# Attention and two mixing blocks on one core: transposes in half-row tiles, and jobs ordered by a table of ranks

## Chip, core and metric

The kernel runs on one NeuronCore of a Trainium2 chip. The metric is device time in microseconds (us), lower is better. The kernel before takes 760.67 us (median of 3 runs, 758.09 to 761.02).

## What is computed

The reference, cut to its three steps (4 batches, 12 heads, 448 positions, head size 64; all float32 but the weights, which come as float64):

```python
scores = scale * np.matmul(q, k.transpose(0, 1, 3, 2))
mask = np.triu(np.ones((seq, seq), dtype=bool), k=1)
...
attn = np.exp(scores)
attn = attn / (np.sum(attn, axis=-1, keepdims=True) + 1e-09)
...
h = np.maximum(xt @ w_tok1, 0.0) @ w_tok2
u = x + h.transpose(0, 2, 1)
h2 = np.maximum(u @ w_ch1, 0.0) @ w_ch2
...
h = np.maximum(x @ w_in, 0.0)
...
u, v = (h[..., :d_ff // 2], h[..., d_ff // 2:])
...
v_n = (v - mu) / np.sqrt(var + 1e-06)
v_s = np.einsum('ts,bsd->btd', w_spatial, v_n) + b_spatial[None, :, None]
gated = u * v_s
return (gated @ w_out).astype(np.float32)
```

## The kernel before, in words

**Jobs and the planner.** The kernel does not write out the order of its instructions. It makes a list of jobs, each with an engine, an estimated duration, the keys that it reads and writes, the buffers that it holds, and a priority (`Plan.job`, L110). `Plan.order` (L134) then simulates the engines (`run`, L197): whenever an engine is free, it takes of the ready jobs the one with the lowest priority value. It does so up to six times; after each pass `due` (L162) works out when each job has to be done at the latest, and these times are the priorities of the next pass. The best of the passes is emitted, and each engine and the one DMA queue (SyncE's, called SP) carries its jobs out in that order, so that a job that waits holds up those behind it on its engine. PSUM banks are given out in this simulation too.

**The stages.** The 48 heads are taken as 24 pairs, n = 0 to 23.
- *Attention.* `scores(n)` (L437) multiplies q and k of both heads of a pair (L497); one head's operands lie in partitions 0 to 63, the other's in 64 to 127, so that each matmul uses half of the array's rows. The queries go in four chunks of 64, 128, 128 and 128. VectorE adds the mask and takes the row maxima (L506), ScalarE takes the exponential and the row sums (L523), VectorE adds 1e-9 to the sums (L534) and inverts them (L535), GpSimd scales the rows (L544). The scores use banks 0 to 3.
- *Transposes.* For n < 17, `transposed(n)` (L553) turns the probabilities with TensorE (L581): 16 blocks of 128 x 128, four to a bank, and each bank is copied to SBUF by ScalarE (L585) or VectorE (L584). From n = 17 on `turned(n)` does it with VectorE and DMAs. The transposes, the weighted sum and the token mixing share banks 4 and 5 (for n < 6 also 6).
- *Weighted sum.* `weighted(n)` (L647) multiplies the turned probabilities with v (L683, L688), each matmul on half of the array's columns, two at once. The result goes to the tile U of the batch.
- *Token mixing* (`token_mix`, L718), after every third pair, and *channel mixing* (`channel`, L861, and for batches 2 and 3 `channel_pair`, L1040, which does seven products in place of eight). Every operand of these products is split in a high and a low float32r part, and a product takes three matmuls (`mm3`, L332: L336 to L338).
- *Gated part* (L1150 on): values, gate, spatial product, projection.

**Weights.** They are loaded as float64 (L381, L1105), turned to float32 by three integer operations on VectorE each (`narrow`, L340: L351, L353, L355), and stored to DRAM (L395, L1107), from where they are loaded again when they are used (L818, L984). The intermediate words lie in PSUM bank 7 for the first eight pieces of the channel weights, and then in bank 3.

## Time and profile before

| what | before |
|---|---|
| time, median of 3 runs | 760.67 us |
| span of the profiled execution | 760.7 us |
| TensorE (PE) busy | 747.2 us, 98% |
| VectorE (DVE) busy | 622.3 us, 82% |
| ScalarE (ACT) busy | 427.4 us, 56% |
| GpSimd (POOL) busy | 298.2 us, 39% |
| moved by DMA | 122.02 MB, mean 160 GB/s |

The profile is that of one execution; its times start at the span's beginning. PE stands for matmuls and PEld for weight loads, which overlap with them. A matmul's own duration is longer than its share of the engine, since matmuls are pipelined: what one costs is read from the start of one to the start of the next. In a timeline, equal instructions that follow each other stand in one line with their number.

### The profile page before, as it was taken

The numbers are of one execution on the slowest core, as the hardware profiler recorded it, in microseconds if no ns is written. First come the engines' busy times: TensorE is split into PE (matmuls) and PEld (weight loads), VectorE is DVE, ScalarE is ACT, GpSimd is POOL, SyncE is SP. The second block draws the span as 40 slices with busy tenths as digits, with TensorE's granted clock in tenths as the row PEclk, the third lists the DMA queues.
The fourth block names the chain that finished last, engine by engine and source line by source line (L and its number), as shares of the span: only waits on it lengthen the run. The fifth ranks groups of instructions, "written<-read, shape, count | busy, mean of one in ns | idle before, by whom it ended". The sixth has DMA issues, their size and how long they took to land. (4 is left out here: it accounts for less than half of the span.)

```text
span 760.7 us, 12440 instructions
## 1 busy us (share of the span) xinstructions
PE 747.2 (98%) x4216; PEld 640.3 (84%) x4216; DVE 622.3 (82%) x1512; ACT 427.4 (56%) x1040; POOL 298.2 (39%) x354
## 2 busy tenths in 40 slices
PE   8999999999989999999999999999999999999998
PEld 4577778888887888888889989998988888888997
DVE  6999599999867878876469978999999897599482
ACT  6998776445347765552336666654573665545241
POOL 4788764265494766563310000000420151542210
PEclk9999999999999999999999999999999999999999
DMA  6687158999976898898823122520301100400213
GB/s 228 207 285 238 55 163 316 335 318 333 339 225 190 298 307 250 234 304 220 241 84 117 39 84 84 187 84 1 118 22 42 43 0 1 132 1 28 83 49 133
DMA packets 48608, 122.02 MB, mean 160 GB/s; under 512 B 4896, under 2 KB 20256, under 8 KB 48032
## 3 DMA queue, kind: packets, MB, share of 16 engines
q1 hardware_dynamic: 48544, 121.23, 48.7%
q8 instruction: 33, 0.54, 0.3%
q14 instruction: 31, 0.25, 0.1%
HBM read 91.46 MB, written 29.75 MB: 159 GB/s over the span
## 5 line engine op out<-in xcount | busy, mean ns | idle before, releaser
L336 PE MATMUL psf<-fb,fa 128*128 128x448 f32 x420 | 154.0, 367 | 1.2 <-DVE hs L1001 0.6
L337 PE MATMUL psf<-fb,fa 128*128 128x448 f32 x420 | 153.7, 366 | 0.0
L338 PE MATMUL psf<-fb,fa 128*128 128x448 f32 x420 | 153.6, 366 | 0.0
L327 POOL TENSOR_TENSOR whl<-whl 128x768 fp32r<-128x768 f32 x45 | 83.2, 1851 | 89.5 <-ACT whl L819 89.4
L523 ACT ACTIVATE P<-P,stats 128x448 f32<-128x448 f32 (+3 forms) x192 | 96.1, 505 | 31.1 <-DVE stats L506 30.8
L544 POOL TENSOR_SCALAR P<-P,stats 128x448 f32<-128x448 f32 (+3 forms) x192 | 88.3, 483 | 38.1 <-DVE stats L535 30.8
L336 PEld LDWEIGHTS psf<-fb,fa 128*128 128x128 f32 x420 | 78.9, 188 | 9.2 <-DVE hs L1001 1.0
L337 PEld LDWEIGHTS psf<-fb,fa 128*128 128x128 f32 x420 | 78.9, 188 | 6.8
L338 PEld LDWEIGHTS psf<-fb,fa 128*128 128x128 f32 x420 | 78.9, 188 | 6.7
L506 DVE CUSTOM_DVE_ANT_0 P<-pss,mask 128x448 f32<-128x448 f32 (+3 forms) x192 | 70.9, 415 | 16.4 <-PE pss L497 16.0
L938 ACT CAST fa<-raw 128x384 fp32r<-128x384 f32 (+1 forms) x112 | 56.4, 531 | 42.7 <-DVE raw L951 21.6
L327 POOL TENSOR_TENSOR wv<-wf,wv 128x512 fp32r<-128x512 f32 x6 | 9.2, 1546 | 153.2 <-ACT wv L1156 153.2
L327 DVE TENSOR_TENSOR fa<-raw,fa 128x384 fp32r<-128x384 f32 (+1 forms) x109 | 61.0, 585 | 7.1 <-ACT fa L938 7.1
L336 PE MATMUL ps<-hid,whl 128*128 128x448 f32 x144 | 55.2, 383 | 3.1 <-DVE hid L330 1.9
L819 ACT CAST whl<-whl 128x768 fp32r<-128x768 f32 x45 | 37.4, 833 | 34.6 <-DMA whl<-plain 33.5
L336 PE MATMUL ps<-uhl,whl 128*128 128x448 f32 x144 | 55.6, 386 | 0.2 <-DVE U L859 0.2
L338 PE MATMUL ps<-hid,whl 128*128 128x448 f32 x144 | 53.3, 370 | 0.0
L337 PE MATMUL ps<-hid,whl 128*128 128x448 f32 x144 | 53.3, 370 | 0.0
L338 PE MATMUL ps<-uhl,whl 128*128 128x448 f32 x144 | 52.7, 366 | 0.0
L337 PE MATMUL ps<-uhl,whl 128*128 128x448 f32 x144 | 52.7, 366 | 0.0
L859 DVE TENSOR_TENSOR U<-ps,U 128x448 f32<-128x448 f32 x48 | 29.5, 619 | 20.9 <-PE ps L338 20.8
L327 POOL TENSOR_TENSOR ql<-stage,qh 128x896 fp32r<-128x896 f32 x18 | 38.1, 2116 | 14.9 <-issue 11.7
(174 smaller groups left out, 1793.2 us busy)
## 6 DMA issues: line engine op xcount, KB each, us to landing
way<-in_wch SPq DMA_DIRECT2D x24, 768.0 KB, 5.7
whl<-plain SPq DMA_DIRECT2D x45, 384.0 KB, 5.0
stage<-in_qkv SPq DMA_DIRECT2D x23, 448.0 KB, 4.7
plain<-way SPq DMA_DIRECT2D x24, 384.0 KB, 6.7
raw<-plain SPq DMA_DIRECT2D x24, 384.0 KB, 3.9
round<-PB SPq DMA_DIRECT2D x7, 1024.0 KB, 6.2
PT<-round SPq DMA_DIRECT2D x28, 256.0 KB, 6.2
v<-in_qkv SPq DMA_DIRECT2D x24, 256.0 KB, 4.1
```

Of the source, the lines that this page charges most:

```text
L327: e.tensor_tensor(lo, x, hi.bitcast(F32), op=ALU.subtract)
L336: nc.tensor.matmul(ps, ah, bh, start=(first and i == 0), stop=False, **kw)
L337: nc.tensor.matmul(ps, ah, bl, start=False, stop=False, **kw)
L338: nc.tensor.matmul(ps, al, bh, start=False, stop=(last and i == n - 1), **kw)
L506: nc.vector.tensor_tensor_reduce(out=P(i)[:M, j, :], in0=ps(i, j), in1=mask[:M, S - 128 : S - 128 + W] if j == 0 and n < BLOCKS or M == 64 ...
L523: nc.scalar.activation(P(i)[:M, j, :], P(i)[:M, j, :], AF.Exp, bias=s.t[:M, 0, c : c + 1], scale=-1.0, accum_out=s.t[:M, 1, c : c + 1])
L544: nc.gpsimd.tensor_scalar(P(i)[:M, j, :], P(i)[:M, j, :], s.t[:M, 2, c : c + 1], 1.0, op0=ALU.mult, op1=ALU.mult)
L819: job("ACT", act(DM, False), lambda: nc.scalar.copy(w.t[:, 0, :], w.t[:, 1, :].bitcast(F32)), r=ks, w=ks, prio=p)
L859: job("DVE", dve(S), lambda d=d, ps=ps: nc.vector.tensor_tensor(u.t[:, d, :], ps.t[:, :S], u.t[:, d, :], op=ALU.add), r=[(ps, 0), *u_keys( ...
L938: job("ACT", act(n, False), lambda: nc.scalar.copy(part(o, 0), at(d)), r=[key(d)], w=[wk], prio=p + 0.1 * o)
```

## The change

1. `transposed` makes two jobs per pair of heads in place of four. Each takes eight blocks, and turns each block in two halves: partitions 0 to 63 into one PSUM bank, partitions 64 to 127 into another, 64 columns each. In all 31 transposes of half a block replace 16 (the last block has one half). The four copies to SBUF have 512, 512, 512 and 448 columns, and write every second group of 64. `weighted` reads the new layout; its first product is cut in 384 and 64 columns.
2. `Plan.order` runs the simulation once, with priorities from a table of ranks that stands in the file, one for each job. The simulation has new durations and delays, counts a switch between full, half-row and half-column matmuls, and prefers to stay in one of these modes. `PASSES` and `due` are gone.
3. The float64 weights lie in DRAM so that each piece that a DMA loads is contiguous as a whole.
4. 1e-9 is put beside each row sum once, at the start, and a `tensor_reduce` adds the two, in place of `tensor_scalar_add`.
5. The conversion of the first eight pieces of channel weights can use bank 7 or 3.

The diff, cut to its core (new durations alone are left out):

```diff
+RANKS = (
...
     def order(self):
...
-        own = {j: (j.eng, j.us, j.emit, j.prio) for j in self.jobs}
-        best = None
-        for k in range(PASSES):
...
+        ranks = array("H", b85decode("".join(RANKS)))
+        assert len(ranks) == len(self.jobs)
+        for j, r in zip(self.jobs, ranks):
+            j.prio = r / 40
+        self.run()
         return sorted(self.jobs, key=lambda j: (j.start, j.index))
...
+            return min(((s, j) for s, j in starts if s <= first + NEAR), key=lambda x: (x[1].prio + (e == "PE" and x[1].mode != mode) * STAY, x[1].index))
...
+            if e == "PE":
+                waited = s > free[e] + 0.03
+                if j.mode != mode and not waited:
+                    s += 0.09
+                if j.mode == 0 and (waited or mode):
+                    us += j.lead
+                mode = j.mode
...
-                nc.vector.tensor_scalar_add(s.t[:, 2, cols], s.t[:, 1, cols], 1e-9)
-                nc.vector.reciprocal(s.t[:, 2, cols], s.t[:, 2, cols])
...
+                nc.vector.tensor_reduce(s.t[:, 1, cols], sums(s)[:, cols, :], axis=mybir.AxisListType.X, op=ALU.add)
+                nc.vector.reciprocal(s.t[:, 1, cols], s.t[:, 1, cols])
...
-        for g in range(4):
-            ps = bank(early if n < NP else banks_tm, "pst")
...
-                for c, src in blocks:
-                    nc.tensor.transpose(ps.t[:, c : c + 128], src, ident)
...
+        t = buf(f"A{n % 2}", [16, 2, 64], F32, "PT")
+        for g in range(2):
+            halves = [bank(early if n < NP else banks_tm, "pst") for _ in range(2)]
+            some = blocks[8 * g : 8 * g + 8]
+
+            def mms(g=g, halves=halves, some=some):
+                for k, (_, src) in enumerate(some):
+                    for r in range(1 if 8 * g + k == 15 else 2):
+                        h = slice(64 * r, 64 * r + 64)
+                        nc.tensor.transpose(halves[r].t[:, 64 * k : 64 * k + 64], src()[h], ident[h, h])
...
+            for r, ps in enumerate(halves):
+                m = 7 if r and g else 8
+
+                def dst(g=g, r=r, m=m):
+                    return t.t[:, 8 * g : 8 * g + m, r, :]
...
-            t0 = t.t[:, 1536 : 1536 + S]
-            for j in range(2):
-                nc.tensor.matmul(ps.t[64 * j : 64 * j + 64, :S], v.t[:, j, :], t0, start=True, stop=False, skip_group_check=True)
+            flat = t.t.rearrange("p k r w -> p (k r w)")
+            for o, w, m in ((64, 384, 1536), (0, 64, 1920)):
+                for j in range(2):
+                    nc.tensor.matmul(ps.t[64 * j : 64 * j + 64, o : o + w], v.t[:, j, :], flat[:, m : m + w], start=(o > 0), stop=(o == 0), skip_group_check=True)
...
-        convert(i % 3 if i < 6 else 1 + i % 2, wch[:, i * DM : i * DM + DM], parts, LOW + i, (7,) if i < 8 else (3,), keep=i)
+        convert(i % 3 if i < 6 else 1 + i % 2, wch[i], parts, LOW + i, (7, 3) if i < 8 else (3,), keep=i)
...
+        nc.gpsimd.memset(sums(s)[:, :, 1:2], 1e-9)
...
+    wch = np.stack([first[u[1]] if u[0] == 1 else second[u[1], u[2]] for u in UNITS])
...
+    wgv = in_pieces(wgv, [HALF] * 8 + [FF] * KM + [HALF] * 8)
+    wtok = in_pieces(wtok, (768, 704, 448))
```

## Rows read from the trace of the kernel before

**Rows 1.** The page's first part: busy us (share) x instructions of each engine.

```profile
PE 747.2 (98%) x4216; PEld 640.3 (84%) x4216; DVE 622.3 (82%) x1512; ACT 427.4 (56%) x1040; POOL 298.2 (39%) x354
```

**Rows 2.** Windows: length, busy us of PE, PEld, DVE, ACT, POOL, granted clock, DMA.

```profile
20.00:40.00 20.00, 18.40 (x139) 11.49 (x137) 18.17 (x82) 20.00 (x65) 15.66 (x30) 1.00 0.69 232
80.00:100.00 20.00, 19.72 (x147) 16.25 (x145) 11.68 (x43) 14.70 (x40) 14.24 (x17) 1.00 0.25 73
180.00:220.00 40.00, 36.74 (x178) 32.30 (x177) 32.88 (x74) 18.23 (x37) 22.96 (x21) 0.96 0.90 310
213.40:216.20 2.80, 2.80 (x9) 2.52 (x8) 2.73 (x6) 2.54 (x4) 2.80 (x5) 0.50 0.54 194
```

**Rows 3.** Waits of TensorE, longest first: us in total, times, longest us.

```profile
PE ps L336 <- DVE hid L330: 1.9, 1, 1.9
...
PE ps L336 <- DVE U L859: 1.2, 2, 1.1
PE psp L1355 <- DVE gate L1363: 0.9, 2, 0.7
```

**Rows 4.** Timeline of TensorE, 212 to 217 us: start, us, instruction.

```profile
212.13 0.47 PE L336 MATMUL ps<-hid,whl 128*128 128x448 f32 x1 [1.94 <-DVE hid L330]
...
213.35 0.58 PE L338 MATMUL ps<-hid,whl 128*128 128x448 f32 x1
...
216.34 0.45 PE L337 MATMUL ps<-hid,whl 128*128 128x448 f32 x1
```

**Rows 5.** Timeline of TensorE, 104 to 106 us: transposes among channel matmuls.

```profile
104.04 1.04 PE L581 MATMUL pst<-ident,P 128*128 128x128 f32 x8
104.84 0.45 PE L336 MATMUL ps<-uhl,whl 128*128 128x448 f32 x1
105.12 0.36 PE L337 MATMUL ps<-uhl,whl 128*128 128x448 f32 x1
105.33 0.37 PE L338 MATMUL ps<-uhl,whl 128*128 128x448 f32 x1
```

**Rows 6.** Timeline of TensorE, 52.8 to 53.3 us: scores in half-row tiles.

```profile
52.86 0.36 PE L497 MATMUL pss<-ql,qh 64*128 64x448 f32 x2
53.06 0.36 PE L497 MATMUL pss<-qh,ql 64*128 64x448 f32 x2
```

**Rows 7.** Timeline of TensorE, 47.7 to 48.5 us: from scores to full matmuls.

```profile
47.78 0.28 PE L497 MATMUL pss<-ql,qh 64*128 64x192 f32 x2
47.89 0.28 PE L497 MATMUL pss<-qh,ql 64*128 64x192 f32 x2
48.10 0.44 PE L767 MATMUL psm<-xs,wt 128*128 128x384 f32 x1
48.38 0.34 PE L768 MATMUL psm<-xs,wt 128*128 128x384 f32 x1
```

**Rows 8.** Weight loads by line and form: busy us, mean ns, idle before.

```profile
L336 PEld LDWEIGHTS psf<-fb,fa 128*128 128x128 f32 x420 | 78.9, 188 | 9.2 <-DVE hs L1001 1.0 <-issue 0.9 <-ACT hs L997 0.2
L581 PEld LDWEIGHTS pst<-ident,P 128*128 128x128 f32 x272 | 30.7, 140 | 7.9 <-POOL P L544 2.6 <-issue 1.5 <-DVE U L787 0.5
```

**Rows 9.** Timeline of TensorE, 109.3 to 109.7 us: from full matmuls to scores.

```profile
109.36 0.37 PE L338 MATMUL ps<-uhl,whl 128*128 128x448 f32 x1
109.65 0.43 PE L497 MATMUL pss<-qh 64*128 64x320 f32 x2
```

**Rows 10.** Timeline of VectorE and of GpSimd, 79.8 to 82.1 us.

```profile
80.33 1.70 DVE L534 TENSOR_SCALAR stats<-stats 128x8 f32<-128x8 f32 x1 [0.31 <-ACT P L523]
79.89 2.11 POOL L327 TENSOR_TENSOR ql<-stage,qh 128x896 fp32r<-128x896 f32 x1
```

**Rows 11.** Timeline of the DMA queue, 69 to 106 us.

```profile
69.69 0.42 SPq L395 DMA_DIRECT2D plain<-way  x1
...
105.18 0.33 SPq L381 DMA_DIRECT2D way<-in_wch  x1
```

**Rows 12.** ScalarE's groups by form: the copy of turned probabilities.

```profile
L585 ACT COPY PT<-pst 128x512 f32<-128x512 f32 x42 | 23.6, 585 | 8.6 <-PE pst L581 8.6
```

More of the change, by code (lines that the diff above doesn't have):

```diff
@@ L1 @@
+from array import array
+from base64 import b85decode
 from contextlib import ExitStack
 from functools import partial
+from itertools import count
 import concourse.bass as bass
@@ L76 @@
+NUMBER = count()
 class Buf:
@@ L81, in __init__ @@
         self.jobs, self.tile, self.left = [], None, 0
+        self.number = next(NUMBER)
     @property
@@ L90, with __init__ @@
 class Job:
-    def __init__(self, eng, us, emit, prio, at, size, index, port, other):
+    def __init__(self, eng, us, emit, prio, at, size, index, port, other, mode, lead):
         self.eng, self.us, self.emit, self.prio, self.at, self.size, self.index = eng, us, emit, prio, at, size, index
-        self.other = other
+        self.other, self.mode, self.lead = other, mode, lead
         self.port = port or eng == "POOL"
@@ L108, in buf, with job @@
         return b
-    def job(self, eng, us, emit, r=(), w=(), touch=(), prio=0.0, at=0.0, size=0, port=False, other=None):
-        j = Job(eng, us, emit, prio, at, size, len(self.jobs), port, other)
+    def job(self, eng, us, emit, r=(), w=(), touch=(), prio=0.0, at=0.0, size=0, port=False, other=None, mode=0, lead=0.1):
+        j = Job(eng, us, emit, prio, at, size, len(self.jobs), port, other, mode, lead)
         for k in r:
@@ L144, in order @@
                 p.after.append(j)
-        own = {j: (j.eng, j.us, j.emit, j.prio) for j in self.jobs}
-        best = None
-        for k in range(PASSES):
-            for j in self.jobs:
-                j.eng, j.us, j.emit, _ = own[j]
-            if not self.run():
-                break
-            end = max(j.start + j.us for j in self.jobs)
-            if best is None or end < best[0]:
-                best = end, [(j.start, j.eng, j.us, j.emit) for j in self.jobs], {b: b.tag for j in self.jobs for b in j.bufs if b.banks}
-            self.due(end, own, k)
@@ L206, in run @@
         engines = ("PE", "ACT", "DVE", "POOL", "SP")
-        free = dict.fromkeys(engines, 0.0)
+        free = dict(zip(engines, (2.5, 2.5, 2.5, 2.7, 0.7)))
         bank_free = [0.0] * 8
         dma = port_free = 0.0
+        mode = 0
         avail = {e: [] for e in engines}
@@ L217, in run, with look @@
                 add(j)
-        def start(j, e):
-            s = max(free[e], j.ready, port_free if j.port else 0.0)
-            for b in j.bufs:
-                if b.banks and b.tag is None:
-                    s = max(s, min(bank_free[i] for i in b.banks))
-            return s
+        def look(e):
+            f, starts, first = free[e], [], inf
+            for j in avail[e]:
+                s = j.ready if j.ready > f else f
+                if j.port and port_free > s:
+                    s = port_free
+                for b in j.banked:
+                    if b.tag is None:
+                        k = sum(c.tag is None and c.banks == b.banks for c in j.banked)
+                        s = max(s, sorted(bank_free[i] for i in b.banks)[k - 1])
+                starts.append((s, j))
+                if s < first:
+                    first = s
+            if first == inf:
+                return None
+            return min(((s, j) for s, j in starts if s <= first + NEAR), key=lambda x: (x[1].prio + (e == "PE" and x[1].mode != mode) * STAY, x[1].index))
         done = 0
@@ L274, in run @@
                     add(a)
-        return True
 @with_exitstack
@@ L368, in mixer_kernel, with sums @@
     job("POOL", 0.1, lambda: None, w=[MASK])
-    stats = [fixed(f"s{i}", [3, 8], F32, f"stats{i}") for i in range(4)]
+    stats = [fixed(f"s{i}", [4, 8], F32, f"stats{i}") for i in range(4)]
+    def sums(s):
+        return s.t[:, 2:4, :].rearrange("p x c -> p (x c)").rearrange("p (c x) -> p c x", x=2)
     small = [fixed(f"p{i}", [512], F32, f"P10{i}") for i in range(2)]
@@ L1036, in seven @@
                     after += start
-                job("PE", 0.607 * n, mms, r=[*after, us[z][1](o), *((*place[o][i][:2], x) for i in range(n) for x in range(2))], w=[(ps, 0)], prio=base + 0.01 * o)
+                job("PE", (0.0, 0.0, 1.216, 1.842)[n], mms, r=[*after, us[z][1](o), *((*place[o][i][:2], x) for i in range(n) for x in range(2))], w=[(ps, 0)], prio=base + 0.01 * o)
                 done(z, o, ps)
```

275 lines of the change are left out of this document (148 added, 127 removed).

## The prediction

> **What bounds the kernel now.** I read the busy shares first. TensorE is busy for 747.2 of 760.7 us [rows 1], so only work taken off TensorE, or time that it loses between its instructions, can shorten the run by much. The windows come second, for where the other engines stand close behind it [rows 2]. From 20 to 40 us ScalarE is busy for 20.00 of 20 us: there the first heads of the attention run alone, and two engines bound them together. From 80 to 100 us VectorE works 11.68 us only, and from 180 to 220 us, where it works 32.88 us, TensorE idles 3.26 us (busy 36.74 of 40). The waits come third, for what TensorE waits for when it does [rows 3]: 1.9 us for one hidden tile of VectorE, 1.2 us for two sums in U, 0.9 us for two gates late in the run. They are few and short, but the longest is not over when the operand comes. TensorE idles 1.94 us before 212.13 us, and from 213.35 to 216.34 us it then takes eight steps of 0.37 us each [rows 4], where the granted clock is 0.50, the lower level of 1.2 GHz [rows 2]. A matmul of that size otherwise takes 0.20 or 0.21 us to the next [rows 5, 6]: 8 x 0.17 = 1.4 us are lost. With the idle 3.26, the stretch from 180 to 220 us loses 4.7 us.
>
> The span and the median of the runs are the same to 0.1 us (760.7 and 760.67), so a sum against the profile is one against the median too.
>
> **The transposes.** 272 of them, 16 for each of the first 17 heads' pairs, run one at a time over the whole array. Eight in a row take 0.80 us to the next matmul, which then takes 0.28 us instead of 0.21 to its successor [rows 5]: 0.87 / 8 = 0.11 us each, and 16 x 0.11 = 1.76 us per head. After the change there are 31, in 16 steps, each of two half-row tiles. That such tiles run at once is seen in the scores: two matmuls of 64 rows with 448 columns start at 52.86, the next two at 53.06 [rows 6], and 0.20 us is what one matmul of 128 rows and 448 columns takes. So a step of 64 columns could take half of 0.11 us, 0.055, if streaming decides. If the weights decide it is dearer: a pair of 192 columns takes 0.11 us (47.78 to 47.89 [rows 7]) where its columns alone would take 0.20 x 192 / 448 = 0.086 us, so a load of 128 weight columns seems to fill 0.11 us there. A transpose's load takes 140 ns, a matmul's 188 [rows 8]; 0.11 less that difference of 0.05 is 0.06 us, and I take 0.06, nearest to a load of its own kind. 16 x 0.06 = 0.96 us, 0.80 us saved per head, 17 x 0.80 = **-13.6 us**. Ends: nothing (0.11 per step) and -15.0 (0.055).
>
> **What the half rows cost at their edges.** A block of half-row matmuls pays on leaving: after 47.89 the next full matmul starts 0.21 us later, and its successor 0.28 later [rows 7], where 0.11 and 0.17 would be the steps; that is 0.21 us in all (a pair of 192 columns takes 0.11, and 384 columns, as here, 0.20 x 384 / 448 = 0.17). On entering, the first pair starts 0.29 us after the last full matmul, at 109.65 for 109.36 [rows 9], 0.09 late. So a block that stands among full matmuls costs 0.30 us, and the old transposes cost nothing there, as the 0.11 above has it all in. Two blocks per head, 34 in all: +10.2 us if every one stands alone. Beside a block of scores they cost nothing, and the edge that stands between scores and transposes today goes: at most two edges a head, one of them entered and one left, 17 x 0.30 = -5 us. In the first 45 us transposes and scores stand side by side, later they stand among channel matmuls; with the planner preferring to stay in a mode, I take **-2 us**. TensorEngine Tiling, of the Trainium skill (Tiling Modes, Key Properties), says that changing the tiling mode drains TensorE; rows 7 agree with 0.1 to 0.2 us an edge. By that rule alone, every block between two drains, the sum would have the 10.2 us just named in place of the -2 and stand near 755.
>
> **What hides the gain at the start.** The first five heads' transposes lie in the stretch where ScalarE is full [rows 2]. Their 5 x 0.80 = 4.0 us may end as TensorE waiting for exponentials; ScalarE's work is not less after the change (four evictions a head before and after). I take **+3 us**; ends 0 and 4.
>
> **The weighted sum.** The first product of each head is cut in 384 and 64 columns: the same columns, but one more pair of loads. At worst a load as long as a transpose's, 140 ns [rows 8], stands free; at best it is hidden: 0 to 2.4 us over 17 heads. I take 0.05 each, **+0.9 us**, nearer to hidden, since loads are busy 84% of the span beside matmuls at 98% [rows 1].
>
> **The constant.** The addition of 1e-9 to eight numbers takes 1.70 us at 80.33 us, and ends at 82.03, with the subtraction on GpSimd that runs from 79.89 to 82.00 [rows 10]: it seems to have waited that one out. If the reduction doesn't, VectorE gains a few us where nobody waits for it; on the path I take 0, between 0 and -2. Its cover is TensorE's other work at that point. The four extra fills of GpSimd at the start come before its first work; 0.
>
> **The order.** It is the one part whose price no row shows, since a table of ranks replaces due dates. What it can get is bounded by the losses: 4.7 us at 180 to 220 us, and the late waits, 0.9 us [rows 3]; at the start, 1.6 us (20 - 18.40) lie idle from 20 to 40 us [rows 2]. There is a means: no weights are loaded for conversion from the store at 69.69 to the load at 105.18 us [rows 11], and VectorE's 8.3 idle us from 80 to 100 lie in this hole; conversions that run there are not late at 193 and 210 us. I take -4.2 of 4.7, -0.8 late, and -1 at the start: **-6 us**; ends -7 and, if the new durations lead the order astray, +7 (the same losses again). New durations in the planner emit nothing themselves; the second bank for conversions goes with the order.
>
> **Weights piece by piece.** The same bytes in closer rows. TensorE's longest waits are for VectorE and none is for a load [rows 3]; so I take 0. If the weights' loads set VectorE's pace from 180 to 220 us, closer rows could give back up to 2 of the 4.7 us, or cost 1 if they are slower.
>
> Sum: 760.7 - 13.6 - 2 + 3 + 0.9 - 6 = **743 us**.
>
> **The rivals.** *The halves bring little.* Steps near 0.11 us, or blocks that mostly stand alone: the transposes then give -3 instead of -12 or so, and with the order's -6 it is 760.7 - 3 - 6 = 752 us. For it: the load-bound pair [rows 7], and a switch at both ends of each block. Against it: the shorter load of a transpose.
>
> *The order gives all.* Blocks put beside scores (-5), all 7 us of losses, the start not hidden: 760.7 - 13.6 - 5 - 7 + 0.9 = 736 us. For it: losses have the same few causes. Against it: every one must be got, on one fixed order.
>
> *The table does nothing.* The ranks are priorities in the same list planner, and could give the old order; only the transposes are left, 760.7 - 13.6 - 2 + 3 + 0.9 = 749 us, between the two above and counted with the first.
>
> *Slower: two banks at once.* Each block of transposes now takes both banks, 4 and 5, that it had one by one; the second block waits until both halves are copied, and so do the sum and the token mixing, which use them too. A copy takes 585 ns [rows 12]; formerly it ran beside the other bank's transposes. If it is exposed at each of the 34 blocks it costs 34 x 0.585 = 19.9 us, against the 13.6 + 2 - 3 - 0.9 = 11.7 us gained and an order that then yields nothing: 769 us. It decides against the change from 11.7 / 19.9 = 59% exposed on. For it: from 45 to 105 us those banks serve nearly everything but scores and channels. Against it: TensorE has channel matmuls on banks 6 and 7 to put between, and rows 3 show no wait of a transpose among the long ones. TensorEngine Tiling (Performance Considerations, PSUM Bottleneck) says that tiling speeds TensorE and not the copies out of PSUM, which may become the bound; no row of before shows that bound.
>
> **How the numbers follow.** The forecast, 743 us, has 0.55; the order giving all 0.15; the halves or the table bringing little 0.18; two banks at once, or an order astray by as much, 0.12. The range, 730 to 756, takes in the first three with their ends and leaves out most of the last and a little below. About 0.5%, 3.8 us, is what a measurement of this kernel can tell from no change, so under 756.9 is faster: 0.55 + 0.15 + 0.13 of the second case = 0.83. Within 0.5%: 0.07; slower: 0.10.
>
> **What would show it.** Transposes at about 0.06 us a step, two starting together, 527 of them for 272. Blocks of them beside scores. No TensorE wait over 1 us at 180 to 220 us, and a granted clock of 1.00 there; VectorE over 15 us busy at 80 to 100 us. ScalarE full, and TensorE idle for some us more, at 20 to 40 us. No reduction as long as 1.70 us. It is wrong if steps take 0.11 us, if TensorE waits for copies of pst, or if channel matmuls wait for weights in more places than now.

## The result: slower by 0.8%, and the profile after

The changed kernel takes 766.47 us (762.8 to 770.52, 6 runs) where the kernel before takes 760.6 in the same comparison (758.09 to 763.44, 6 runs): 1.0084 times the time, 95% interval 1.0060 to 1.0108. The forecast was 743. The profiled execution of the changed kernel took 764.43 us, and the span from its first to its last instruction is 762.6. That is 1.9 us more than the span of before, 760.7, and the accounts below explain these 1.9. The other 4.0 of the 5.9 us between the medians stand in no trace: the profiled execution of the change lies 2 us under its median, and that of before must lie some 2 us over its own, since every run on record takes at least 1.7 us more than its span.

The page's first part and the windows of TensorE, after (length, busy us, granted clock, DMA):

```profile
PE 742.3 (97%) x4539; PEld 631.8 (83%) x4539; DVE 620.9 (81%) x1527; ACT 423.5 (56%) x1025; POOL 290.5 (38%) x358
```

```profile
0.00:100.00 100.00, 94.37 (x870) 1.00 0.75 249
...
180.00:220.00 40.00, 39.78 (x312) 1.00 0.78 262
220.00:320.00 100.00, 97.94 (x699) 1.00 0.84 262
320.00:340.00 20.00, 17.58 (x97) 0.91 0.92 248
...
640.00:700.00 60.00, 55.65 (x259) 1.00 0.14 46
700.00:760.00 60.00, 59.06 (x286) 1.00 0.23 84
```

The same view of the kernel before, where [rows 2] did not show it:

```profile
0.00:100.00 100.00, 95.67 (x686) 1.00 0.60 197
...
220.00:320.00 100.00, 99.75 (x666) 1.00 0.83 259
320.00:340.00 20.00, 20.00 (x137) 1.00 0.92 268
...
640.00:700.00 60.00, 59.10 (x281) 1.00 0.16 50
700.00:760.00 60.00, 57.11 (x282) 0.99 0.22 85
```

TensorE's busy time fell by 4.9 us [rows 1], and its idle time rose by more than that. The old loss from 180 to 220 us is gone: 0.22 us idle for 3.26, at clock 1.00. It has come back elsewhere: 2.42 us idle from 320 to 340 (before: none), 2.06 from 220 to 320 (0.25), 4.35 from 640 to 700 (0.90), 5.63 in the first 100 us (4.33). Of the other stretches shown only the last gains, 0.94 for 2.89.

The transposes themselves do what was forecast. The timeline of TensorE, after:

```profile
47.85 0.71 PE L621 MATMUL pst<-ident,P 64*128 64x64 f32 x16
48.50 0.47 PE L377 MATMUL psm<-wt,hid 128*128 128x448 f32 x1
48.81 0.36 PE L378 MATMUL psm<-wt,hid 128*128 128x448 f32 x1
...
52.05 0.36 PE L379 MATMUL psm<-wt,hid 128*128 128x448 f32 x1
52.34 0.71 PE L621 MATMUL pst<-ident,P 64*128 64x64 f32 x16
52.86 0.45 PE L541 MATMUL pss<-qh 64*128 64x448 f32 x2
```

Eight pairs take 0.52 us up to the scores that follow (52.34 to 52.86): 0.065 us a pair, where a whole block took 0.11 [rows 5]. A full matmul begins 0.65 us after the block's start (47.85 to 48.50), and its successor 0.31 later, where 0.52 and 0.20 would be the steps: 0.24 us for leaving. Entering costs 0.29 for 0.20 (52.05 to 52.34). An edge on both sides is 0.33 us; 0.30 was the estimate.

TensorE's longest waits, after:

```profile
PE psm L377 <- DVE xs L368: 2.1, 1, 2.1
PE psp L1409 <- DVE gate L1417: 1.7, 1, 1.7
PE psp L1409 <- DVE gate L1055: 1.4, 1, 1.4
...
PE pst L621 <- DVE hid L371: 1.2, 1, 1.2
PE psm L795 <- DVE xs L368: 1.2, 2, 1.0
...
PE pso L734 <- ACT PT L635: 0.8, 1, 0.8
PE psm L795 <- DVE PT L634: 0.8, 1, 0.8
```

There are more of them than in [rows 3], in other places: 15.6 us in all that the view lists, for 9.2 before. The first can be followed back. The timelines of the DMA queue, ScalarE, VectorE and TensorE around it:

```profile
321.17 0.33 SPq L872 DMA_DIRECT2D whl<-plain  x1
...
321.57 0.86 ACT L804 CAST xs<-psm 128x384 fp32r<-128x384 f32 x2
327.82 0.83 ACT L873 CAST whl<-whl 128x768 fp32r<-128x768 f32 x1 [5.39 <-DMA whl<-plain]
328.56 0.47 ACT L802 CAST xs<-psm 64x384 fp32r<-64x384 f32 x1
...
329.43 1.14 DVE L368 TENSOR_TENSOR xs<-psm,xs 128x384 fp32r<-128x384 f32 x2 [2.62 <-ACT xs L804]
...
330.05 0.47 PE L377 MATMUL psm<-wt,hid 128*128 128x448 f32 x1 [2.14 <-DVE xs L368]
...
331.82 0.71 PE L377 MATMUL ps<-hid,whl 128*128 128x448 f32 x1 [0.29 <-DVE U L913]
332.33 0.57 PE L378 MATMUL ps<-hid,whl 128*128 128x448 f32 x1
...
334.95 0.45 PE L379 MATMUL ps<-hid,whl 128*128 128x448 f32 x1
```

The waits name VectorE, but the cause lies further back. A load of plain weights is issued at 321.17 and has landed at 327.75 (the chain of waits in that stretch puts "DMA whl<-plain" at 6.57 us). ScalarE stands before it with its cast for 5.39 us, and the casts of `xs`, which need no load, stand behind that cast in ScalarE's queue. VectorE waits for them. TensorE's matmul at 330.05 doesn't read `xs` at all: it writes a token product, and waits for one of the two banks, 4 and 5, which holds a piece of `xs` until VectorE is done with it. So the late load reaches TensorE through a bank. After 2.14 us idle and another 0.29 it takes steps of 0.37 us from 332.33 to 334.95, at a granted clock of 0.50: the same aftermath as [rows 4], moved by 119 us.

Two more of the waits listed go back to a load in the same way. The transposes at 149.90 us wait 1.03 us for a bank with `xs`, and those at 238.18 wait 1.24 us for one with `hid`. Before the former ScalarE stood before a load, and before the latter VectorE stood 1.85 us before another:

```profile
146.88 0.83 ACT L873 CAST whl<-whl 128x768 fp32r<-128x768 f32 x1 [2.62 <-DMA whl<-plain]
```

Waits that end when one of those banks is given free, and not when an operand comes, make up 5.9 us of the 15.6; before it was 1.1:

```profile
PE pst L581 <- ACT PT L585: 0.5, 1, 0.5
PE pst L581 <- ACT U L692: 0.3, 1, 0.3
PE pst L581 <- DVE U L787: 0.3, 1, 0.3
```

The two waits for a gate, 1.7 and 1.4 us at 673 and 692 us, are of another kind: VectorE is busy for 31.41 of the 32.3 us from 660 on, and nothing is loaded there (DMA share 0.00).

Over the whole run, each TensorE instruction counted from its start to the next start, in us (worked out from all starts in the two traces; of full matmuls what they take beyond 0.203 us for 448 columns, and in proportion for others):

| | before | after |
|---|---|---|
| transposes of P | 32.8 | 22.7 |
| full matmuls, waits over 0.13 us (count) | 7.3 (10) | 13.6 (19) |
| full matmuls, step into another mode (count) | 2.2 (24) | 3.5 (37) |
| full matmuls, first step after a mode or wait | 7.2 | 7.7 |
| full matmuls, small deviations of the step | 1.7 | 4.4 |
| full matmuls, steps at the lower clock | 1.4 | 1.5 |
| scores / weighted sums / token transposes | 50.7 / 52.9 / 11.2 | 50.4 / 53.3 / 11.9 |

The transposes give 10.1 us. The full matmuls take 6.3 back in waits, 1.8 at edges and 2.7 in their steps. A row holds what follows its last instruction as well: in the changed kernel, waits behind three blocks of transposes, with 0.55, 1.07 and 1.05 us from the last start to the next. Inside the blocks a whole transpose took 0.114 us and a half takes 0.034, so that the steps alone, 272 and 527 of them, give 13.3 us.

### The profile page after: what moved, and what is told of

It reads as the page before. It is cut to its first block, busy times and chain, and to the rows that moved or that the text cites. A ratio compares the mean times of both kernels' runs of the same rounds, so it can differ in the third digit from the quotient of the medians.

```text
span 762.6 us, 13072 instructions
## 1 busy us (share of the span) xinstructions
PE 742.3 (97%) x4539; PEld 631.8 (83%) x4539; DVE 620.9 (81%) x1527; ACT 423.5 (56%) x1025; POOL 290.5 (38%) x358
## 4 chain that ended last, share of the span: by engine, by line
PE 59%; DVE 19%; DMA 9%; ACT 3%; issue 2%; SPq 0%; DVEq 0%; ACTq 0%
PE psf L377 9%; PE psf L378 9%; PE psf L379 9%; PE ps L377 6%; PE ps L378 5%; PE ps L379 5%; DMA whl<-plain 3%; PE pss L541 2%; DMA gw<-in_wgv 2%; PE pso L719 2%; PE psm L377 2%; DMA way<-in_wch 1%; PE psm L379 1%; PE psm L378 1%; DVE psw L392 1%
## 5 line engine op out<-in xcount | busy, mean ns | idle before, releaser
L567 ACT ACTIVATE P<-P,stats 128x320 f32<-128x320 f32 (+3 forms) x192 | 96.3, 503 | 19.6 <-DVE stats L550 19.2
L588 POOL TENSOR_SCALAR P<-P,stats 128x320 f32<-128x320 f32 (+3 forms) x192 | 87.7, 473 | 34.1 <-DVE stats L579 23.9
L550 DVE CUSTOM_DVE_ANT_0 P<-pss,mask 128x320 f32<-128x320 f32 (+3 forms) x192 | 71.6, 412 | 7.3 <-PE pss L541 7.1
L378 PE MATMUL ps<-hid,whl 128*128 128x448 f32 x144 | 53.3, 370 | 0.0
L379 PE MATMUL ps<-hid,whl 128*128 128x448 f32 x144 | 53.3, 370 | 0.0
L379 PE MATMUL ps<-uhl,whl 128*128 128x448 f32 x144 | 52.8, 367 | 0.0
L378 PE MATMUL ps<-uhl,whl 128*128 128x448 f32 x144 | 52.8, 366 | 0.0
```

Of the source, the lines that this page charges most:

```text
L378: nc.tensor.matmul(ps, ah, bl, start=False, stop=False, **kw)
L379: nc.tensor.matmul(ps, al, bh, start=False, stop=(last and i == n - 1), **kw)
L550: nc.vector.tensor_tensor_reduce(out=P(i)[:M, j, :], in0=ps(i, j), in1=mask[:M, S - 128 : S - 128 + W] if j == 0 and n < BLOCKS or M == 64 ...
L567: nc.scalar.activation(P(i)[:M, j, :], P(i)[:M, j, :], AF.Exp, bias=s.t[:M, 0, c : c + 1], scale=-1.0, accum_out=sums(s)[:M, c, 0:1])
L588: nc.gpsimd.tensor_scalar(P(i)[:M, j, :], P(i)[:M, j, :], s.t[:M, 1, c : c + 1], 1.0, op0=ALU.mult, op1=ALU.mult)
```

## The experiments

Each time is a median, and each ratio is to runs of the kernel before on the same chip, with its 95% interval. Different groups of runs were on different chips, where the kernel before takes 760.2 to 760.9 us. A difference between groups is good to 1 or 2 us: by the ratios, the 8.4 us of `e4_whole` below are 7.1, the 8.9 of `e8_due_pace` 7.6, the 6.4 of `e17_scalar` 5.5 and the 6.2 of `e21_half_loads` 6.9.

### The halves or the order

`e1_half` is the kernel before with half rows and the recut weighted sum alone; its planner learns that a job may need two banks:

```diff
-        for g in range(4):
-            ps = bank(early if n < NP else banks_tm, "pst")
+        for g in range(2):
+            halves = [bank(early if n < NP else banks_tm, "pst") for _ in range(2)]
...
-                    s = max(s, min(bank_free[i] for i in b.banks))
+                k = sum(c.banks == b.banks for c in need)
+                s = max(s, sorted(bank_free[i] for i in b.banks)[k - 1])
```

> The kernel before with the half-row transposes alone (and the weighted sum that reads them), ordered by the old planner. Dear halves (the new blocks, their two banks and their edges cost as much as they save): 760 to 768 us, transposes' steps near 0.06 us but TensorE waiting for copies of pst or U. Order at fault (the halves are sound, what was lost lies in the new order): 750 to 757 us, 4 to 10 below before.

Measured: 777.1 us, 1.0201 (1.0177 to 1.0226), slower than either theory had it. TensorE's waits in the view come to 26.2 us, for 9.2 before, and the copies of P and what is queued with them appear in the list:

```profile
PE pst L584 <- DVE hid L337: 3.4, 2, 2.6
...
PE pst L584 <- DVE PT L597: 2.0, 2, 1.6
PE pst L584 <- ACT PT L598: 1.9, 2, 1.4
```

`e2_old_planner` has everything of the change but the order (the planner and its due dates are those of before):

```diff
-        ranks = array("H", b85decode("".join(RANKS)))
+        own = {j: (j.eng, j.us, j.emit, j.prio) for j in self.jobs}
+        best = None
+        for k in range(PASSES):
```

> The kernel after in all but its order: half-row transposes, the reduction, the contiguous weights and the second bank for conversions, ordered by the old planner with due dates and its old durations. Dear halves: 760 to 768 us, as after. Order at fault: 748 to 756 us, and the waits of TensorE fall back from 13.6 us to near the 7.3 of before.

Measured: 766.46 us, 1.0066 (1.0041 to 1.0090), the time of the changed kernel. So the table, taken as a whole, brought nothing over the old planner.

`e4_whole` keeps the change's order job by job and turns whole blocks, into the same two banks, with the same copies:

```diff
-                    for r in range(1 if 8 * g + k == 15 else 2):
-                        h = slice(64 * r, 64 * r + 64)
-                        nc.tensor.transpose(halves[r].t[:, 64 * k : 64 * k + 64], src()[h], ident[h, h])
+                    o = halves[k // 4].t[:, 128 * (k % 4) :]
+                    nc.tensor.transpose(o[:, :128], src(), ident)
```

> The kernel after with its order kept job by job, but the blocks turned whole (128 rows, 128 columns each, two banks as after, the same copies): the halves alone undone. Dear halves: no slower than after, 758 to 766 us. Order at fault: TensorE has 17 x 0.8 = 13.6 us more to do, less at most 34 x 0.3 = 10 us of edges and what falls into waits: 768 to 776 us.

Measured: 774.88 us, 1.0178 (1.0153 to 1.0203): 8.4 us more than the change. With the order fixed, the half rows are worth 8.4 us; they are not dear.

`e7_due_new` is the change with due dates, as before, in place of the table, in the change's model of durations:

```diff
-        ranks = array("H", b85decode("".join(RANKS)))
+        for k in range(PASSES):
...
+            self.due(end, own)
```

> The kernel after with due dates in place of the table of ranks, in the planner's new model of durations, delays and loads. The plan's own end is 740.4 us, for 739.0 with the table. Table brittle (a searched order fits the model only, due dates leave room): 745 to 754 us. Model at fault (loads land on the chip 0.6 us later than the new model has them, so that any order made by it waits): 758 to 768 us, with TensorE waits over 10 us again.

Measured: 766.47 us, 1.0068 (1.0029 to 1.0108). An order that no search has touched takes the same time in the same model, so the time does not hang on the table as such. The losses lie elsewhere, though: from 640 to 700 us nothing is idle here, where the change loses 4.35 us.

### Two banks, or loads that come late

Two suspects were left: that a block of transposes takes both banks, and that the change's model counts on loads faster than they are.

`e10_two_banks` is `e1_half` with whole blocks (the lines of `e4_whole`), in the same order of jobs, so that the two banks are left without the half rows. The recut weighted sum stays too:

```diff
-                        nc.tensor.transpose(halves[r].t[:, 64 * k : 64 * k + 64], src()[h], ident[h, h])
+                    nc.tensor.transpose(halves[k // 4].t[:, 128 * (k % 4) :][:, :128], src(), ident)
```

> The kernel before, its own planner and order, with one thing of the change alone: a job turns eight blocks, whole as before, into both banks 4 and 5 at once, and two copies carry them off (before: four blocks, one bank). No half rows. Theory 'Two banks at once': the same kernel with half rows took 777.1 us, and under the new order whole blocks cost 8.4 us more than half rows, so 777 + 8 = 785 us (776 to 792), with TensorE's first transposes of a job and the weighted sums waiting for the copies of P, 15 us and more of waits in all. Theory 'Half rows cost it' (the turns between modes and what the half rows do to the matmuls beside them made the 777.1): taking both banks costs nothing, 757 to 764 us.

Measured: 778.92 us, 1.0258 (1.0233 to 1.0284). The kernel before, planned again for two banks, loses 18 us without a half row in it, as the first theory had it. But its waits for copies of P come to 2.6 us only, where 15 and more were expected for the banks. The runs that exchange the constant, below, divide this further. Not all of it is a wait for banks. Its plan ends at 755.7 us, where that of the kernel before ends at 749.1, and it counts a job of eight blocks at 0.7 us, where eight whole blocks take 8 x 0.11 = 0.88 [rows 5].

`e11_old_wide` is `e2_old_planner` with five banks to choose from:

```diff
-halves = [bank(early if n < NP else banks_tm, "pst") for _ in range(2)]
+halves = [bank(early if n < NP else [4, 5, 0, 1, 2], "pst") for _ in range(2)]
```

> The change without its order (that took 766.5 us), and its transposes may use five banks (0, 1, 2, 4, 5) where the change leaves them two (4, 5). Theory 'Two banks at once': the waits for copies of P, of xs and for the weighted sum's bank shrink from some 12 us to 4 or less, 754 to 760 us, faster than the kernel before. Theory 'Loads too early or late': banks are not the matter, 764 to 769 us, with the scores' matmuls waiting in place of the channel ones, since banks 0 to 2 are theirs.

Measured: 759.01 us, 0.9991 (0.9977 to 1.0005): 7.5 us less than with two banks, within the forecast of the first theory, though no faster than before beyond the interval.

`e8_due_pace` is `e7_due_new` with slower loads in the planner. It and `e9_due_wide` may also make more passes, 20 and 12 for 6, but both emit their second, so nothing hangs on that:

```diff
-... + j.size / (j.lead * 1e6)
+... + j.size / (0.82 * j.lead * 1e6)
```

> The change with due dates in place of its table (766.5 us) and its model's pace of the loads taken down to 0.82, which is what the landings of the trace of the change ask for. Its plan ends 11 us later than the unpaced one. Theory 'Loads': what the plan gave up comes back on the chip, 753 to 760 us, and ACT's wait for the plain copies of the weights falls from 62 us to 35 or less. Theory 'Two banks at once': late loads are a part of under 3 us, 764 to 772 us.

Measured: 757.55 us, 0.9968 (0.9955 to 0.9982): 8.9 us less. The group of ScalarE's casts of these weights, first of the changed kernel, then of this one (busy us, mean ns, idle before and what ended it):

```profile
L873 ACT CAST whl<-whl 128x768 fp32r<-128x768 f32 x45 | 37.5, 833 | 61.9 <-DMA whl<-plain 61.9
```

```profile
L856 ACT CAST whl<-whl 128x768 fp32r<-128x768 f32 x45 | 37.2, 832 | 28.4 <-DMA whl<-plain 27.3 <-POOL P L571 1.0
```

The wait fell from 62 to 27 us, as the theory of the loads asked; in `e7_due_new` it was 58.8. The loads themselves did not change. The view of the changed kernel's loads has, as a median from issue to landing, 5.1 us; here and in the kernel before it is 5.0:

```profile
whl<-plain SPq DMA_DIRECT2D x45, 384.0 KB, 5.1
```

The planners counted 6.2 us for them before, 4.1 in the change and 8.0 here (medians of the simulations in the three kernels). So the expectation is wrong that the landings ask for 0.82: it overshoots them by far. What helps is an order that leaves room for late loads, as that of before does; that the figure be right is not shown.

`e9_due_wide` is `e7_due_new` with five banks for transposes, weighted sums and token matmuls:

```diff
-halves = [bank(early if n < NP else banks_tm, "pst") for _ in range(2)]
+halves = [bank(early if n < NP else [4, 5, 0, 1, 2], "pst") for _ in range(2)]
...
-        ps = bank(early if n < NP else banks_tm, "pso")
+        ps = bank(early if n < NP else [4, 5, 0, 1, 2], "pso")
...
-                tm = early if g < 2 else banks_tm
+                tm = early if g < 2 else [4, 5, 0, 1, 2]
```

> The change with due dates in place of its table (766.5 us), and transposes, weighted sums and token matmuls may use banks 0, 1, 2, 4 and 5 in place of 4 and 5; the model of the loads as in the change. Its plan ends 1 us later than the one on two banks. Theory 'Two banks at once': 753 to 760 us, waits of TensorE under 8 us in place of 14. Theory 'Loads': 764 to 769 us, the waits are still there and stand at other instructions.

Measured: 765.85 us, 1.0085 (1.0064 to 1.0107). With the loads counted too fast, banks change nothing that the interval tells. So the two suspects are both real, each where the other does not stand in front: under the old planner, which leaves room for the loads, the banks; under the change's planner, the loads.

### The loads alone, in the same order

`e21_half_loads` keeps the change's order and cuts one load; `e23_before_half_loads` does the same to the kernel before.

```diff
-nc.sync.dma_start(w.t[:, 1, :].bitcast(F32), plain[i])
+nc.sync.dma_start(w.t[:, 1, : DM // 2].bitcast(F32), plain[i][:, : DM // 2])
```

> The change, job for job in its order, but the 45 loads of plain weights (whl, 384 KB each) bring only the first half of the columns; ScalarE's cast reads them twice, and GpSimd subtracts the cast from itself, so every instruction but the load is of the same size. Part of the computation is left out: the second half of each unit's weights and all their low parts. Theory 'Loads': ScalarE's wait for these loads falls from 62 us to some 30, TensorE's wait of 2.1 us at 328 us goes, 757 to 762 us. Theory 'Two banks at once alone': 764 to 767 us.

> The control: the same cut in the kernel before, job for job in its order (the same part of the computation left out). Theory 'Loads': its planner counted with loads that land 1 us later than they do, so shorter ones give it little: 758 to 760.5 us. If shorter loads help any order alike, the gain here is that of the change's order: 751 to 756 us, and the loads say nothing of the change.

Measured: 760.27 us for the change (0.9993, 0.9966 to 1.0019), 6.2 less than whole; 758.33 for the control (0.9972, 0.9960 to 0.9985), 2.4 less than before. ScalarE's wait in the former:

```profile
L880 ACT CAST whl<-whl 128x768 fp32r<-128x768 f32 x45 | 37.1, 831 | 44.3 <-DMA whl<-plain 44.2
```

It fell by less than expected (44 us, not 30), but TensorE's wait of 2.1 us for `xs` is 0.9 here. Any order gains something from shorter loads; the change's gains 3.8 us more than that of before, with an uncertainty of about 3 us by the intervals. The late waits for gates are as they were in the change, so the loads are not their cause:

```profile
PE psp L1416 <- DVE gate L1424: 1.7, 1, 1.7
...
PE psp L1416 <- DVE gate L1062: 1.4, 1, 1.4
...
PE psm L377 <- DVE xs L368: 0.9, 1, 0.9
```

### The parts alone

`e16_strided` is the change with the weights laid out as before, in the same order of jobs:

```diff
-convert(..., wch[i], ...)
+convert(..., wch[:, i * DM : i * DM + DM], ...)
...
-piece(wgv, o, n).bitcast(U32)
+wgv[:, o : o + n].bitcast(U32)
```

> The change with one part undone, the layout of the input weights (column slices of one wide matrix, as before); job for job the same order. Theory 'The layout helps the loads': the weights' loads take 0.2 to 0.7 us longer to land, as before, and under an order that already waits for loads that is 2 to 6 us: 768 to 773 us. Theory 'The layout is nothing': 765 to 768 us.

Measured: 765.66 us, 1.0075 (1.0048 to 1.0102). The layout makes no difference that these runs can tell, as the prediction had it.

`e17_scalar` is the change with the constant added as before, in the same order of jobs:

```diff
-nc.vector.tensor_reduce(s.t[:, 1, cols], sums(s)[:, cols, :], axis=mybir.AxisListType.X, op=ALU.add)
+nc.vector.tensor_scalar_add(s.t[:, 1, cols], sums(s)[:, cols, 0], 1e-9)
```

> The change with one part undone: the constant is added by a tensor_scalar in place of the tensor_reduce, job for job the same order. Theory 'It waits for GpSimd': some 5 of its 25 instances last over 0.4 us, up to 2 us, each ending with an instruction of GpSimd that runs as it starts, where the reduction's longest lasted 0.171 us; DVE loses some 4 us, and 0 to 2 us of it reach the end: 766 to 769 us. Theory 'It was chance in one order': all 25 last about 0.17 us, 766.5 us within 1.

Measured: 772.93 us, 1.0156 (1.0129 to 1.0183): 6.4 us more than the change, far above what was expected of it. The instruction in the changed kernel, then here (ns, shortest, median, longest), then GpSimd and VectorE here at one of the long ones:

```profile
L578 DVE TENSOR_REDUCE stats<-stats x25: 144/158/171, 8.9 to 320.9; 128x8 f32<-128x16 f32 x23, 128x4 f32<-128x8 f32 x2
```

```profile
L578 DVE TENSOR_SCALAR stats<-stats x25: 144/165/2514, 8.4 to 331.2; 128x8 f32<-128x8 f32 x23, 128x4 f32<-128x4 f32 x2
```

```profile
157.40 0.33 POOL L588 TENSOR_SCALAR P<-P,stats 64x64 f32<-64x64 f32 x1
157.51 2.32 DVE L578 TENSOR_SCALAR stats<-stats 128x8 f32<-128x8 f32 x1
...
157.68 2.13 POOL L368 TENSOR_TENSOR ql<-stage,qh 128x896 fp32r<-128x896 f32 x1
```

Eight of the 25 last over 0.4 us, and each ends 0.03 us after an instruction of GpSimd that ran meanwhile, here at 159.83 and 159.81. In the lines shown, GpSimd was at one instruction when VectorE's began, and VectorE's waited out the next one too. None of the short ones lies inside an instruction of GpSimd, while ten of the 25 reductions in the changed kernel do, and take no longer for it. VectorE loses 10.9 us (14.8 for 4.0 in all 25), everything that needs the inverted sums waits with it, and the end moves by 6.4.

`e18_reduce`, `e19_two_reduce` and `e20_half_reduce` put the same reduction into the kernel before, into `e10_two_banks` and into `e1_half`, each job for job in its order:

```diff
-nc.vector.tensor_scalar_add(s.t[:, 2, cols], s.t[:, 1, cols], 1e-9)
+nc.vector.tensor_reduce(s.t[:, 1, cols], sums(s)[:, cols, :], axis=mybir.AxisListType.X, op=ALU.add)
```

> The kernel before with the tensor_reduce in place of the tensor_scalar, job for job the same order. In the trace of before the tensor_scalar's five long instances cost VectorE 3.7 us. Theory 'Paid by the microsecond': under the change's order 10.9 us of VectorE saved were worth 6.4 us, so 3.7 us are worth some 2 us: 757.5 to 759.5 us. Theory 'Only where an order depends on it': 760 to 761.5 us, no difference.

> The kernel with whole blocks turned into two banks (778.9 us, its tensor_scalar 17.2 us of VectorE in 25), with the tensor_reduce alone added, job for job the same order. Theory 'Mostly the constant': 13.3 us of VectorE come back, at the rate of the change's order 8 us of the end: 769 to 773 us, so that taking two banks costs some 10 us by itself. Theory 'Mostly the banks': 776 to 779 us, and the waits of TensorE at pst, pso and psm are as they were.

> The kernel with half rows turned into two banks (777.1 us, its tensor_scalar 16.9 us in 25), with the tensor_reduce alone added, job for job the order of the kernel before it in this list. Theory 'Mostly the constant': 767 to 771 us. Theory 'Mostly the banks': 774 to 777 us. Against the kernel with whole blocks: the half rows' steps alone, 16 x 17 x 0.045 = 12 us at most by the steps; in this order the two with the tensor_scalar lay 1.8 us apart, and if the wait for the copies takes what the steps give, it is 2 us again.

Measured: 759.28 us, 0.9993 (0.9977 to 1.0010); 772.46 us, 1.0166 (1.0125 to 1.0207); 770.15 us, 1.0121 (1.0090 to 1.0153). The reduction is worth 1.3 us in the order of before, which the interval does not tell from nothing, and 6.5 and 7.0 in the other two. There the old instruction took 17 us in 25, so of the 18 us of `e10_two_banks` a good third was the constant. From 759.3 to 772.5, 13 us, are left for the two banks, with the recut sum and the plan that ends 6.5 us later. In that order the half rows seem to win 2.3 of them back, which the intervals do not tell from nothing. These 13 are those of one re-planned order, whose profiled execution was its longest (778.0 us): TensorE's waits for copies of P are only 1.0 us of its waits in it, and which of the others follow from the banks was not followed up one by one.

### A version that beats both

`e14_table_pace` is the change with its table searched anew under the slower loads of `e8_due_pace`; `e15_table_pace_wide` and `e13_pace_wide` add the five banks of `e11_old_wide`, with a table and with due dates:

```diff
-RANKS = ( the table of the change )
+RANKS = ( a table searched anew )
...
-... + j.size / (j.lead * 1e6)
+... + j.size / (0.82 * j.lead * 1e6)
```

> The change itself (half rows, its two banks, its table in form), with two edits: the planner's pace of the loads is 0.82 of the change's, and the table of ranks is searched anew under that pace. Its plan ends at 743.5 us, where the change's own ends at 739.0. Theory 'Loads': what was wrong with the table was the model that it was searched in; the due dates at this pace lagged behind their plan by 4.7 us (plan 751.1, span 755.8) with 1.8 us around the span, so 743.5 + 4.7 + 1.8 = 750 us (747 to 754). Theory 'A searched order is tight': an order with the slack squeezed out loses some 20 us on the chip whatever the loads do, as the change's did (plan 739.0, span 762.6): 762 to 767 us.

> As the kernel before it in this list, and the transposes may also use banks 0, 1 and 2 beside 4 and 5; its table is searched for that, and the plan ends at 740.7 us. Theory 'Loads and banks both': 740.7 + 4.7 + 1.8 = 747 us (744 to 751), and TensorE waits for copies of P at transposes under 2 us in all. Theory 'A searched order is tight': 759 to 765 us. If the banks are no matter once the loads are paced: the same as the one with two banks within 2 us.

> The change with due dates for its table, the loads' pace at 0.82 (757.6 us with two banks) and five banks for the transposes. Its plan ends at 750.7 us, that of two banks at 751.1. Theory 'Loads and banks both': the waits for copies of P at the transposes (1.2 us) and for P (3.0 us) are what the banks could give: 753 to 756 us. Theory 'The banks matter only where the loads' pace is right by itself already': 757 to 760 us, no better.

Measured: 757.44 us, 0.9955 (0.9938 to 0.9972); 757.96 us, 0.9967 (0.9949 to 0.9986); 760.71 us, 1.0002 (0.9984 to 1.0020). All three missed what the theories of the loads, and of loads and banks both, gave them, and the two tables lie short of their rivals' 762 and 759 too. The banks add nothing once the loads are paced, as two of the three expectations allowed. The new table lags 13 us behind its plan (743.5, span 756.5), the wider one 18 (740.7, span 759.1, in its longest execution; some 15 by its median), where the due dates lag 4.7: a search under the slower pace of loads took 7.6 us out of the plan and none out of the chip. What makes those two lag is open. `e8_due_pace` and `e14_table_pace` are the fastest, 3 us under the kernel before. Where the rest of the half rows' gain stays in `e8_due_pace`, its windows show:

```profile
0.00:100.00 100.00, 90.20 (x823) 1.00 0.72 241
...
640.00:700.00 60.00, 60.00 (x287) 1.00 0.17 59
```

The hole from 640 to 700 us is closed, as it was in `e7_due_new`, and the first 100 us hold 9.8 idle us for 4.3 before. So some 5 us are lost at the attention's start; that the other engines bind there, as the prediction had it, is likely and not shown for this order.

## Why the prediction was wrong

It forecast 743 us, and the kernel takes 766.5; the range ended at 756. Against the profiled spans the sum forecast -17.7 us and +1.9 came. That a sum against the profile is one against the median too was a misreading: the span of 760.7 and the median of 760.67 agree by chance, as the profiled execution of before must have taken about 2 us more than its span. By its steps:

**The transposes**, -13.6: right. Two halves start together, 527 transposes stand for 272, a pair takes 0.065 us where 0.06 was taken, and the steps inside the blocks give 13.3. With what follows each block the start-to-start sum fell by 10.1, and with the order fixed the half rows are worth 8.4.

**The edges**, -2: the price of an edge was right, 0.33 for 0.30, and of 39 blocks 29 now touch a block of scores (25 of 45 before). But the old transposes stood among full matmuls in the same mode, and the new ones do not: a full matmul steps into another mode in 37 places without a wait, for 24 before, and the edges came to +1.8. The count was wrong, not the price. The rule of the Trainium skill (TensorEngine Tiling, Tiling Modes, Key Properties) that a change of mode drains TensorE agrees with the 0.33 us; the 10.2 us that it would have made, with every block alone, did not come.

**The start**, +3: right in kind, too large for this order. ScalarE and VectorE are busy 19.77 us each from 20 to 40 us, and TensorE falls to 17.92 us from 18.40 [rows 2]; over the first 100 us its idle time grew by 1.3.

**The weighted sum**, +0.9: +0.4 by the sums. **The layout**, 0: 0.8 us between `e16_strided` and the change, within the intervals.

**The constant**, 0 with an end of -2: right for the kernel before (-1.3, undecided), wrong for the change, where it saves 6.4 us. The step read five long instances as a matter of that trace. They are one of whatever GpSimd runs at that moment, so another order makes other numbers: 7.7 us of VectorE before, 14.8 in the change's order, 16.9 in `e1_half`.

**The order**, -6: this is the step that failed. Its losses were read correctly, and the largest was even got: VectorE works 18.35 us from 80 to 100 us (11.68 before), as the prediction asked, and nothing waits over 1 us from 180 to 220 us. But "what it can get is bounded by the losses" has no bound for what it can lose, beyond a +7 named as the same losses again. An order is made against a model, and this model counts 4.1 us for a plain load that lands after 5.1, where the old one counted 6.2. Full matmuls wait 6.3 us more where 6 less were forecast: 12 of the 19.6 us between the forecast and the spans. `e8_due_pace` (-8.9 by the pace alone) and `e21_half_loads` (-6.2, -3.8 beyond its control, in the same order) show that an order without room for its loads is the larger part of it. A smaller part is the table's own: the waits for gates from 640 to 700 us, 4.0 us for 0.9 before, stay when the loads are cut and are gone with due dates; why the table has VectorE late there is open.

**Two banks at once** was a rival, at 769 us, and its price in the sum was 0. Its number is the nearest to the result, and under the old planner its claim holds: 13 us. It was ruled unlikely because "rows 3 show no wait of a transpose"; but there each job took one bank and left the other free, so those rows could not show it. In the changed kernel itself TensorE waits only 1.6 us for copies of P, far from an exposed copy at 59% of 34 blocks, so that its number is near is luck. Its banks have a part all the same: TensorE's waits for banks 4 and 5 rose from 1.1 to 5.9 us, and the three longest of them, 4.4 us, are where a late load came through. Five banks without slower loads gave 0.6 us (`e9_due_wide`), shorter loads with two banks 6.2, so the loads decide. That the half rows need two banks at all stands in TensorEngine Tiling of the Trainium skill (Restrictions and Gotchas, Gotcha 1): row tiles write to different banks and raise the pressure on PSUM. These runs agree, with up to 13 us beside it in one order.

**The steps of full matmuls**, not in the sum at all: +2.7 us, below. And 4.0 us lie between the medians beyond the 1.9 between the spans, which no trace here explains.

Not shown: how the 26.2 us of waits in `e1_half` divide among its banks, its constant and its order instruction by instruction, and why a searched order lags behind its plan by more than due dates do.

## What to carry to other kernels

An order fixed at build time needs room for its loads: before believing a plan, compare its landings with the trace's, and look for an engine that stands in its queue before a load with work behind it that needs none. When tiles are split to run at once, count the PSUM banks that they now hold together, and don't read the lack of a wait in the old trace as room, since the old form could not have shown it. A wait that names an engine's tile can be one for the bank that the tile still holds: look whether the waiting instruction reads it. An instruction whose time depends on what a neighbour engine does has no fixed price, and its price moves with every reordering.

## What the runs showed of the hardware

**This small `tensor_scalar` on VectorE waits out GpSimd; `tensor_reduce` doesn't.** 8 of 25 took 0.46 to 2.5 us in `e17_scalar` where the reduction's longest was 0.171, though ten of the reductions ran inside an instruction of GpSimd. VectorE: DVE Perf Modes of the Trainium skill ("The perf-mode tier table") has a reduction run in the basic mode alone, and advises ("Rules for kernel authors") to restructure where one is on a hot path; by that the exchange would have been a loss. Here its median is 158 ns for 165, and it saved 6.4 us. The page gives single-source fp32 work a mode that uses both read ports ("Mode 2×_2P"), the second of them shared with GpSimd ("Two Vector instructions with no wait between them"); that fits the ends of the long instances, but no run here tells the mode.

**Full matmuls have two steps, 0.2027 and 0.2067 us, and keep one for long.** The changed kernel, before and in a long stretch of full matmuls, then `e8_due_pace` in the same stretch:

```profile
692.26 0.48 PE L1409 MATMUL psp<-wsp,gx 128*128 128x448 f32 x1 [1.45 <-DVE gate L1055]
...
714.68 0.37 PE L377 MATMUL psf<-fb,fa 128*128 128x448 f32 x1
...
731.83 0.37 PE L378 MATMUL psf<-fb,fa 128*128 128x448 f32 x1
```

```profile
714.54 0.36 PE L360 MATMUL psf<-fb,fa 128*128 128x448 f32 x1
...
731.97 0.36 PE L360 MATMUL psf<-fb,fa 128*128 128x448 f32 x1
```

In the first, 83 steps take 17.15 us, 0.2066 each; in the second, 86 take 17.43, 0.2027 each, with the same tiles, the same size and the granted clock at 1.00. In the changed kernel the slow step sets in some matmuls after the wait that ends at 692.26 and lasts for over 300 of them; the stretch before that wait ran at the fast one. Over some 2,300 such matmuls all at the one or all at the other are 2,300 x 0.004 = 9 us apart, so which step a stretch falls into is worth as much as many an edit. What chooses it stays open.
